# Pooling the first image with half the products, and another order of the work before the main loop

## The chip, the cores and the metric

The program runs on one core of one Trainium2 chip. The metric is the time of one execution on the device in microseconds (us); the median of several runs counts. The profile's names for the engines are PE (TensorE's products), PEld (TensorE's weight loads), DVE (VectorE), ACT (ScalarE), POOL (GpSimd) and SP (SyncE, which issues all transfers here).

## What is computed

Four images of 12,288 queries with 128 channels attend to keys that are pooled from a 384x32 map, and the result goes through a wide layer and back.

```
kv_pool = kv.reshape(B, H // r, r, W // r, r, C).mean(axis=(2, 4))   # r = 4
k = v = kv_pool.reshape(B, -1, C) @ w_sr                             # 768 keys
s = scale * (q @ k.T);  s = s - s.max(-1)
a = exp(s);  a /= a.sum(-1) + 1e-09
x = a @ v                                                            # (49152, 128)
h = x @ w_in                                                         # 2048 wide
out = (0.5 * h * (1 + erf(h / sqrt(2)))) @ w_out                     # 128 wide
```

## The kernel before

**Tiles.** The 49,152 queries are 96 tiles of 512; a tile has four chunks c of 128 queries. The layer's 2048 columns are 16 groups f of 128. All large products are made in float16 with each operand split in a high and a low half, three products for one: `score` (L408, and L439 in halves) for queries by keys, `av_first` (L510) and `av` (L524) for attention by values, `mlp_in` (L543 to L545) and `mlp_out` (L574 to L576) for the layer.

**One tile's path.** `q_max` (L360) and `q_scale` on VectorE find a scale for the queries, `q_split` on GpSimd (L381 to L383) makes the halves, `q_turn` transposes them by a transfer (L389). `score` writes a score chunk, `evac` (L419; `evac_half` L451) takes it out on VectorE with its extreme, `exp` runs on ScalarE (L462), `recips` (L475) makes reciprocals, `attn_hi` and `attn_lo` (L482, L486) make the halves of the attention, `attn_turn` (L495) transposes them by a transfer. `x_out` (L534, L535) makes the layer's input from the product with the values. `gelu` (L557, L559) and `rest` (L563) stand between the layer's two products. `rest(t, p)` serves the groups 2p and 2p + 1.

**Before the first tile.** The first image's map comes in twelve pieces `kv_load(j)` of 512 KB. A piece holds, for each of 128 map rows, two windows w of four pixels e. `kv_pool` (L199) multiplies each pixel's 128x128 float32 block, as the stationary operand, by a 128x32 matrix that averages groups of four rows, and adds four pixels in PSUM. After four pieces ScalarE copies the group out (`kv_copy`, L206), `kv_key` (L212) multiplies by w_sr, and `kv_max` (L218) takes the maximum on VectorE. A short chain on VectorE and TensorE (`kv_bound`, L283 to L297) makes a scale, and `kv_high` and `kv_low` (L303, L308) make the keys' halves.

**The weights.** They arrive as 64-bit numbers in eight chunks, four of w_in (j = 0 to 3) and four of w_out (4 to 7). `w_max` (L632) reads each, `w_scale(i, step)` makes the scale of each matrix, and `w_split(j, step)` makes the two float16 halves in five steps: 0 and 2 on ScalarE (L692, L693, L703), 1 (L695 to L701), 3 (L705, L706) and 4 (L709, L710) on VectorE. Two chunks share one of two staging tiles, so the output weights' transfers wait until the input chunks there have been read.

**What sets the order.** Nothing reorders the work: each engine runs its instructions in the order in which the Python code issues them, and waits only on data and buffers. A list `START` gives that order by hand up to the first layer input of tile 1; behind it a loop over i (tile) and f (group) issues the layer of tile i along with scores and attention of the tiles after it, and `mlp_out` six groups later (`LAG`). In the loop's first turn, i = 1, the dictionary `SECOND` places scores left over from `START`:

```
for name, *a in START:
    by[name](*a)
for i in range(1, NT + 1):
    for f in range(FB if i < NT else LAG):
        if i < NT:
            mlp_in(i, f)
            gelu(i, f)
        if i == 1 and f in SECOND:
            score(*SECOND[f])
            evac(*SECOND[f])
```

## Time and profile before

| | |
|---|---|
| median of 3 runs | 2867.42 us (2867.06 to 2867.5) |
| profiled execution | 2868.9 us, span of the profile 2867.1 us |
| TensorE busy | 2806.6 us (98%) |
| ScalarE busy | 2530.4 us (88%) |
| VectorE busy | 2360.2 us (82%) |
| GpSimd busy | 844.3 us (29%) |

The span runs from the first to the last instruction. Busy shares are averages over the whole of it; the loop over 95 tiles makes up most.

### The profile page before, as it was taken

What the parts mean: (1) busy time and instruction counts of PE and PEld (TensorE: products, weight loads), DVE (VectorE), ACT (ScalarE), POOL (GpSimd) and SP (SyncE); (2) the same over time, 40 slices, a digit from 0 to 9 for tenths busy, and PEclk for the clock granted to TensorE, in tenths of its full rate; (3) what the DMA queues carried; (4) which work ended last, traced back from release to release, by engine and by line L of the source; (5) the groups of instructions that cost most, each with busy time, mean ns of one, the idle gap of its engine ahead of it and who ended that gap; (6) DMA issues with size and microseconds to landing.
All of it is one profiled execution on the core that took longest, in us unless ns stands there. A gap on an engine that the chain in (4) does not pass through costs nothing.

```text
span 2867.1 us, 37928 instructions
## 1 busy us (share of the span) xinstructions
PE 2806.6 (98%) x13570; PEld 1354.0 (47%) x13570; DVE 2360.2 (82%) x3533; ACT 2530.4 (88%) x3416; POOL 844.3 (29%) x801
## 2 busy tenths in 40 slices
PE   7689999999999999999999999999999999999999
PEld 6244444444444444444444444444444444444444
DVE  4778888788878888889788888888878787878785
ACT  2589989898999999999999999999999999999997
POOL 0133433323234334332323344423231323232221
PEclk9899999999999999999999999999999999999999
...
GB/s 176 52 108 117 106 106 112 90 89 101 94 105 109 101 116 116 97 87 103 87 100 98 116 115 109 104 100 85 102 91 100 85 100 85 100 84 101 91 90 48
DMA packets 852990, 284.91 MB, mean 99 GB/s; under 512 B 814656, under 2 KB 817088, under 8 KB 852800
## 3 DMA queue, kind: packets, MB, share of 16 engines
...
q14 instruction: 84, 0.69, 0.1%
...
## 4 chain that ended last, share of the span: by engine, by line
PE 90%; DVE 4%; issue 4%; ACT 1%; DMA 0%; POOL 0%; SPq 0%; POOLq 0%; DVEq 0%; ACTq 0%
PE s L408 12%; PE px L524 12%; PE po L574 11%; PE po L576 11%; PE po L575 11%; PE h L545 11%; PE h L544 11%; PE h L543 11%; DVE gl L563 1%; DVE a L486 1%; DVE a L482 1%; ACT sn L462 1%; DVE sn L419 1%; ACT L462 0%; DMA q<-in_q_dram 0%
## 5 line engine op out<-in xcount | busy, mean ns | idle before, releaser
L557 ACT ACTIVATE g<-h,hs 128x512 f32<-128x512 f32 x1536 | 1006.1, 680 | 235.5 <-PE h L545 214.4
L563 DVE SCALAR_TENSOR_TENSOR gl<-g,gs,gh 128x1024 f16<-128x1024 f32 x768 | 1007.7, 1315 | 39.0 <-ACT gh L559 37.5
L559 ACT ACTIVATE gh<-g,gs 128x1024 f16<-128x1024 f32 x768 | 881.9, 1148 | 25.0
L575 PE MATMUL po<-gl,wo_h 128*128 128x512 f16 x1536 | 582.7, 379 | 4.0 <-DVE gl L563 4.0
L543 PE MATMUL h<-xh,wi_h 128*128 128x512 f16 x1536 | 583.9, 380 | 2.1 <-ACT g L557 1.2
L574 PE MATMUL po<-gh,wo_h 128*128 128x512 f16 x1536 | 582.9, 379 | 2.3 <-ACT oT L581 2.2
L381 POOL TENSOR_TENSOR q<-q,qi 128x512 f32<-128x512 f32 x96 | 100.1, 1043 | 1646.1 <-DVE qi L373 1646.1
L544 PE MATMUL h<-xl,wi_h 128*128 128x512 f16 x1536 | 583.9, 380 | 0.8 <-DVE xl L535 0.8
L545 PE MATMUL h<-xh,wi_l 128*128 128x512 f16 x1536 | 583.9, 380 | 0.0
L576 PE MATMUL po<-gh,wo_l 128*128 128x512 f16 x1536 | 582.6, 379 | 1.1 <-DVE wo_l L710 1.1
L408 PE MATMUL s<-k,q_v 128*128 128x384 f16 x2274 | 434.1, 327 | 25.7 <-DMA q_v<-q_u 12.7
L419 DVE TENSOR_SCALAR_CACHE_REDUCE sn<-s,sg 128x768 f32<-128x768 f32 x379 | 383.7, 1012 | 85.9 <-PE s L408 82.8
L486 DVE SCALAR_TENSOR_TENSOR a<-sn,r,a 128x768 f16<-128x768 f32 x384 | 405.7, 1057 | 13.5
L524 PE MATMUL px<-aT,v 128*128 128x512 f16 x1710 | 416.8, 380 | 0.0
L462 ACT ACTIVATE sn<-sn,nm 128x768 f32<-128x768 f32 x384 | 354.5, 924 | 11.6 <-DVE sn L419 8.9
L408 PEld LDWEIGHTS <-q_v 128*128 128x128 f16 x2274 | 222.5, 98 | 217.1 <-issue 18.2
L524 PEld LDWEIGHTS <-v 128*128 128x128 f16 x1710 | 167.7, 98 | 203.7 <-issue 3.4
L475 DVE TENSOR_SCALAR r<-sum 128x2 f32<-128x2 f32 (+2 forms) x192 | 39.4, 205 | 262.9 <-ACT sn L462 262.9
L482 DVE TENSOR_SCALAR a<-sn,r 128x768 f16<-128x768 f32 x377 | 248.2, 658 | 6.8 <-DVE r L478 0.3
L576 PEld LDWEIGHTS <-wo_l 128*128 128x128 f16 x1536 | 150.4, 98 | 187.7 <-issue 4.4
L545 PEld LDWEIGHTS <-wi_l 128*128 128x128 f16 x1536 | 150.6, 98 | 183.5 <-issue 3.3
L544 PEld LDWEIGHTS <-wi_h 128*128 128x128 f16 x1536 | 150.6, 98 | 179.2 <-issue 4.1
...
## 6 DMA issues: line engine op xcount, KB each, us to landing
...
kv<-in_kv_dram SPq DMA_DIRECT2D x12, 512.0 KB, 9.3
aT<-a SPq DMA_TRANSPOSE x384, 3.2
w<-in_moe_w_in_dram SPq DMA_DIRECT2D x4, 512.0 KB, 5.6
w<-in_moe_w_out_dram SPq DMA_DIRECT2D x4, 512.0 KB, 7.7
q_v<-q_u SPq DMA_TRANSPOSE x96, 2.8
```

Of the source, the lines that this page charges most:

```text
L408: nc.tensor.matmul(ps[:, n, :KH], lhs[:, c], rhs[:, n * KH : (n + 1) * KH], start=rhs is kh and lhs is qh, stop=lhs is ql,)
L486: nc.vector.scalar_tensor_tensor(a[:, 1, :], st.pop(("s", t, c)), st["r", t][:, c : c + 1], a[:, 0, :], op0=ALU.mult, op1=ALU.subtract,)
L524: nc.tensor.matmul(ps, v[:, w, :], aT[:, :, o + k, :], start=k == 0 and i == 0, stop=k == KB - 1 and i == 2,)
L543: nc.tensor.matmul(ps, wi_h[:, fs], xh, start=True, stop=False)
L544: nc.tensor.matmul(ps, wi_h[:, fs], xl, start=False, stop=False)
L545: nc.tensor.matmul(ps, wi_l[:, fs], xh, start=False, stop=True)
L557: nc.scalar.activation(g[:, e, :], ps, AF.Gelu, scale=st["hs", b])
L559: nc.scalar.mul(gh, g, st["gs", b])
L563: nc.vector.scalar_tensor_tensor(gl, st["g", t, p], st["gs", t // TPB], st["gh", t, p], op0=ALU.mult, op1=ALU.subtract)
L574: nc.tensor.matmul(ps, wo_h[:, f, :], gh[:, e, :], start=f == 0, stop=False)
L575: nc.tensor.matmul(ps, wo_h[:, f, :], gl[:, e, :], start=False, stop=False)
L576: nc.tensor.matmul(ps, wo_l[:, f, :], gh[:, e, :], start=False, stop=f == FB - 1)
```

## The change

Four things change, all before or in the loop's first turn.

- A new step `kv_add(j)` adds pixels 2 and 3 of each window to pixels 0 and 1 on VectorE, in place, and `kv_pool` multiplies two blocks a window instead of four.
- The weight steps stand elsewhere: chunks 0 to 2 between the additions, the rest of chunk 2 behind the layer's scale, the rest of chunk 3 among the first tile's layer. The maxima of the output chunks move forward.
- In the first tile, attention chunk 3 is turned and multiplied before chunk 2. The queries of tiles 2 and 3 are scaled earlier, the scores of tile 2 and their exponentials stand in `START`, and so do all products of `mlp_out` of tile 0.
- The loop's first turn starts with the reciprocals of tile 2, and leaves out what `START` now has.

```diff
-    ("w_split", 0, 1), ("w_scale", 0, 2), ("kv_pool", 0), ("w_split", 0, 2), ("w_split", 0, 3),
...
+    ("w_split", 0, 1), ("kv_add", 0), ("kv_pool", 0), ("kv_add", 1), ("kv_pool", 1),
+    ("w_scale", 0, 2), ("w_split", 0, 2), ("kv_add", 2), ("kv_pool", 2), ("w_split", 0, 3),
...
-SECOND = {0: (2, 2), 2: (2, 3), 4: (3, 0), 6: (3, 1), 8: (3, 2), 9: (3, 3)}
+SECOND = {4: (3, 1), 7: (3, 2), 9: (3, 3)}
...
+    def kv_add(j):
+
+        t = st["kv0", j]
+        nc.vector.tensor_tensor(t[:, :, :2], t[:, :, :2], t[:, :, 2:], op=ALU.add)
+
...
-            for e in range(R):
+            for e in range(2):
                 nc.tensor.matmul(
                     st["pp", j // 4][:, o : o + n], t[:, w, e], group,
-                    start=e == 0, stop=e == R - 1,
+                    start=e == 0, stop=e == 1,
                 )
...
-                    if 0 <= k < NT * FB // 2:
+                    if FB // 2 <= k < NT * FB // 2:
                         rest(k // (FB // 2), k % (FB // 2))
-                if i == 1 and f == 3:
-                    exps(2)
+                if i == 1 and f == 0:
                     recips(2)
-                if i == 1 and f in (4, 5, 6, 7):
-                    attn(2, f - 4)
+                    attn(2, 0)
+                    evac(3, 0)
+                if i == 1 and f in (1, 3, 5):
+                    attn(2, (f + 1) // 2)
...
-                    if 0 <= m < NT * FB and (m == n) == (m % FB > 0):
+                    if FB <= m < NT * FB and (m == n) == (m % FB > 0):
                         mlp_out(m // FB, m % FB)
```

The new code stands above most functions, so line numbers rise by 12: L199 becomes L211, L360 becomes L372, L563 becomes L575.

TensorE, the end of the first group's pooling and the first key product, before (`pp` is the pooled group, `kv_j` piece j, `pk` the key product):

```order
L199 MATMUL pp_0_232<-group,kv_2_150 128x32 x8
L199 MATMUL pp_0_232<-group,kv_3_152 128x32 x8
L199 MATMUL pp_1_281<-group,kv_4_154 128x32 x8
L212 MATMUL pk_0_291<-pT_0_276,w_sr_sb 128x256
L199 MATMUL pp_1_281<-group,kv_5_156 128x32 x8
```

The same place in the changed kernel:

```order
L211 MATMUL pp_0_226<-group,kv_2_150 128x32 x4
L211 MATMUL pp_0_226<-group,kv_3_152 128x32 x4
L211 MATMUL pp_1_263<-group,kv_4_154 128x32 x4
L224 MATMUL pk_0_269<-pT_0_256,w_sr_sb 128x256
L211 MATMUL pp_1_263<-group,kv_5_156 128x32 x4
```

The products of a piece are halved, and the order of the pieces and of the key product is the same.

VectorE, from the first weight chunk's selection (`wt`) on, before:

```order
L701 SCALAR_TENSOR_TENSOR wt_193<-wt_193 128x512
L274 TENSOR_REDUCE rho_m<-rho_ps 128x1
L670 TENSOR_SCALAR rmax<-rho_m 128x1
L671 RECIPROCAL xs<-rho_m 128x1
L672 TENSOR_SCALAR xs<-xs,rho 128x1
L705 TENSOR_SCALAR wt_193<-wt_193 128x512
L706 TENSOR_TENSOR wt_193<-wt_193 128x512
L695 TENSOR_SCALAR wt_197<-w_137 128x512
```

and in the changed kernel:

```order
L713 SCALAR_TENSOR_TENSOR wt_193<-wt_193 128x512
L200 TENSOR_TENSOR kv_0_146<-kv_0_146 128x2x256
L200 TENSOR_TENSOR kv_1_148<-kv_1_148 128x2x256
L286 TENSOR_REDUCE rho_m<-rho_ps 128x1
L682 TENSOR_SCALAR rmax<-rho_m 128x1
L683 RECIPROCAL xs<-rho_m 128x1
L684 TENSOR_SCALAR xs<-xs,rho 128x1
L200 TENSOR_TENSOR kv_2_150<-kv_2_150 128x2x256
L717 TENSOR_SCALAR wt_193<-wt_193 128x512
L718 TENSOR_TENSOR wt_193<-wt_193 128x512
L200 TENSOR_TENSOR kv_3_152<-kv_3_152 128x2x256
L707 TENSOR_SCALAR wt_197<-w_137 128x512
```

The additions (L200) stand between the weight steps, and the products of piece j wait for addition j.

VectorE, around the maximum of tile 2's queries (`qm`) in the first tile's layer (`gl` is the result of `rest`, `a` the attention, `sn` scores taken out), before:

```order
L563 SCALAR_TENSOR_TENSOR gl_5_824<-g_10_804,gs_419,gh_10_805 128x1024
L709 SCALAR_TENSOR_TENSOR wt_701<-wt_701,inv_684,wo_h 128x512
L710 SCALAR_TENSOR_TENSOR wo_l<-wt_701,inv_684 128x512
L486 SCALAR_TENSOR_TENSOR a_3_826<-sn_3_638,r_704,a_3_826 128x768
L360 TENSOR_REDUCE qm_842<-q_189 128x4
L369 TENSOR_SCALAR qm_842<-qm_842 128x4
L370 TENSOR_SCALAR qe_844<-qm_842 128x4
L373 TENSOR_SCALAR qi_845<-qe_844 128x4
L397 TENSOR_SCALAR sg_855<-qe_844,ks_401 128x4
L563 SCALAR_TENSOR_TENSOR gl_6_868<-g_12_837,gs_419,gh_12_838 128x1024
L419 TENSOR_SCALAR sn_0_889,nm_887<-s_0_880,sg_855 128x768
```

and in the changed kernel:

```order
L721 SCALAR_TENSOR_TENSOR wt_491<-wt_491,inv_630,wo_h 128x512
L722 SCALAR_TENSOR_TENSOR wo_l<-wt_491,inv_630 128x512
L372 TENSOR_REDUCE qm_662<-q_189 128x4
L381 TENSOR_SCALAR qm_662<-qm_662 128x4
L382 TENSOR_SCALAR qe_664<-qm_662 128x4
L385 TENSOR_SCALAR qi_665<-qe_664 128x4
L575 SCALAR_TENSOR_TENSOR gl_1_680<-g_2_641,gs_379,gh_2_642 128x1024
L498 SCALAR_TENSOR_TENSOR a_0_660<-sn_0_496,r_649,a_0_660 128x768
L409 TENSOR_SCALAR sg_687<-qe_664,ks_360 128x4
L707 TENSOR_SCALAR wt_634<-w_183 128x512
```

The maximum stood behind the sixth `rest` and the last output chunk; it now stands behind the first output chunk and before the second `rest`. The first scores of tile 2 are taken out with 20 rows between, where two rows stood between before.

## Rows read from the trace of the kernel before

**Rows 1.** Busy time in stretches: us, then busy us of PE, PEld, DVE, ACT, POOL (instructions), PEclk.
```profile
12.54:55.26 42.72, 42.72 (x197) 42.22 (x196) 18.66 (x37) 4.16 (x8) 2.80 (x3) 1.00 0.52 179
55.26:81.14 25.88, 17.08 (x124) 10.28 (x125) 18.03 (x60) 13.56 (x25) 0.00 (x0) 1.00 0.47 87
81.14:163.82 82.68, 50.14 (x198) 20.78 (x198) 60.79 (x103) 48.21 (x65) 13.56 (x11) 0.83 0.24 59
...
300.00:1500.00 1200.00, 1198.87 (x5817) 570.57 (x5816) 1020.08 (x1508) 1095.39 (x1477) 382.69 (x357) 1.00 0.44 101
```

**Rows 2.** TensorE in order of time, pooling: start, us, what, [idle before <-releaser].
```profile
12.54 17.11 PE L199 MATMUL pp<-group,kv 128*128 128x32 f32 x80
29.47 1.20 PE L212 MATMUL pk<-pT,w_sr_sb 128*128 128x256 f32 x2
30.46 13.70 PE L199 MATMUL pp<-group,kv 128*128 128x32 f32 x64
...
55.78 1.22 PE L212 MATMUL pk<-pT,w_sr_sb 128*128 128x256 f32 x2 [0.52 <-ACT pT L206]
```

**Rows 3.** VectorE in order of time, same columns: first weight chunk, last key maximum.
```profile
13.02 0.69 DVE L701 SCALAR_TENSOR_TENSOR wt<-wt 128x512 f32<-128x512 f32 x1
...
57.45 0.42 DVE L218 TENSOR_REDUCE mx<-pk 128x1 f32<-128x256 f32 x1 [10.20 <-ACT kT L213]
```

**Rows 4.** VectorE's waits from 81.14 to 163.82: us in total, times, longest us.
```profile
DVE sn L419 <- PE s L408: 7.9, 2, 6.7
DVE r L475 <- ACT sn L462: 6.1, 1, 6.1
DVE xh L534 <- PE px L524: 5.5, 1, 5.5
```

**Rows 5.** TensorE in order of time: scores behind its two longest gaps.
```profile
124.54 2.10 PE L408 MATMUL s<-k,q_v 128*128 128x384 f16 x6 [11.97 <-DMA q_v<-q_u]
...
163.82 1.36 PE L408 MATMUL s<-k,q_v 128*128 128x384 f16 x6 [4.10 <-DVE sn L419]
```

**Rows 6.** GpSimd in order of time: the split of tile 2's queries, and a later one's start.
```profile
117.87 1.04 POOL L381 TENSOR_TENSOR q<-q,qi 128x512 f32<-128x512 f32 x1 [67.60 <-DVE qi L373]
...
120.54 1.15 POOL L383 TENSOR_TENSOR q_u<-q,q_u 128x512 f16<-128x512 f32 x1
...
154.14 1.34 POOL L381 TENSOR_TENSOR q<-q,qi 128x512 f32<-128x512 f32 x1 [13.28 <-DVE qi L373]
```

**Rows 7.** Groups of VectorE's instructions, 81.14 to 163.82: busy us, mean ns | idle before.
```profile
L709 DVE SCALAR_TENSOR_TENSOR wt<-wt,inv,wo_h 128x512 f32<-128x512 f32 x4 | 3.0, 744 | 0.0
...
L706 DVE TENSOR_TENSOR wt<-wt 128x512 f32<-128x512 f32 x4 | 2.8, 692 | 0.2
...
L632 DVE TENSOR_REDUCE wm<-w 128x1 f32<-128x512 f32 x3 | 1.9, 678 | 0.0
...
L705 DVE TENSOR_SCALAR wt<-wt 128x512 int32<-128x512 int32 x4 | 1.7, 420 | 0.0
```

**Rows 8.** VectorE in order of time: `rest` without and beside a split on GpSimd.
```profile
149.92 1.28 DVE L563 SCALAR_TENSOR_TENSOR gl<-g,gs,gh 128x1024 f16<-128x1024 f32 x1
...
157.16 1.92 DVE L563 SCALAR_TENSOR_TENSOR gl<-g,gs,gh 128x1024 f16<-128x1024 f32 x1
```

**Rows 9.** The page's transfers: count, KB each, median us from issue to landing.
```profile
kv<-in_kv_dram SPq DMA_DIRECT2D x12, 512.0 KB, 9.3
aT<-a SPq DMA_TRANSPOSE x384, 3.2
```

**Rows 10.** VectorE in order of time: first score, last weight maximum before x_out(0), x_out(0).
```profile
63.74 1.02 DVE L419 TENSOR_SCALAR_CACHE_REDUCE sn<-s,sg 128x768 f32<-128x768 f32 x1 [0.70 <-PE s L408]
...
78.29 0.68 DVE L632 TENSOR_REDUCE wm<-w 128x1 f32<-128x512 f32 x1
...
81.14 0.75 DVE L534 TENSOR_SCALAR xh<-px,xs 128x512 f16<-128x512 f32 x1 [2.17 <-PE px L510]
```

**Rows 11.** The page's costliest groups: the exponential.
```profile
L462 ACT ACTIVATE sn<-sn,nm 128x768 f32<-128x768 f32 x384 | 354.5, 924 | 11.6 <-DVE sn L419 8.9
```

More of the change, by code (lines that the diff above doesn't have):

```diff
@@ L55 @@
-    ("av_first", 0, 2), ("av_first", 0, 3), ("w_max", 4), ("x_out", 0), ("evac", 1, 3),
-    ("exp", 1, 3), ("mlp_in", 0, 0), ("gelu", 0, 0), ("mlp_in", 0, 1), ("gelu", 0, 1),
-    ("w_max", 5), ("w_max", 6), ("w_max", 7), ("w_scale", 1, 0), ("w_split", 6, 0),
-    ("w_scale", 1, 1), ("w_split", 4, 1), ("mlp_in", 0, 2), ("gelu", 0, 2), ("w_scale", 1, 2),
-    ("out_scale",), ("w_split", 4, 3), ("rest", 0, 0), ("w_split", 4, 2), ("mlp_in", 0, 3),
-    ("gelu", 0, 3), ("w_split", 4, 4), ("w_split", 7, 0), ("recips", 1, 0, 4), ("mlp_in", 0, 4),
@@ L61 @@
-    ("gelu", 0, 4), ("rest", 0, 1), ("w_split", 5, 1), ("mlp_in", 0, 5), ("gelu", 0, 5),
-    ("attn_hi", 1, 0, "act"), ("w_split", 5, 3), ("w_split", 5, 2), ("rest", 0, 2),
-    ("mlp_out", 0, 0), ("mlp_in", 0, 6), ("mlp_out", 0, 1), ("gelu", 0, 6), ("w_split", 5, 4),
-    ("attn_lo", 1, 0), ("attn_turn", 1, 0), ("mlp_out", 0, 2), ("mlp_in", 0, 7), ("gelu", 0, 7),
-    ("w_split", 6, 1), ("rest", 0, 3), ("attn_hi", 1, 1, "act"), ("mlp_out", 0, 3),
-    ("mlp_in", 0, 8), ("w_split", 6, 3), ("w_split", 6, 2), ("gelu", 0, 8), ("attn_lo", 1, 1),
@@ L73 @@
-    ("q_split", 2), ("q_turn", 2), ("q_sigma", 2), ("q_load", 3), ("mlp_out", 0, 8),
-    ("mlp_in", 0, 13), ("gelu", 0, 13), ("rest", 0, 6), ("mlp_out", 0, 9), ("mlp_in", 0, 14),
-    ("gelu", 0, 14), ("score", 2, 0), ("evac", 2, 0), ("mlp_in", 0, 15), ("gelu", 0, 15),
-    ("av", 1, 0), ("av", 1, 1), ("av", 1, 2), ("x_out", 1), ("score", 2, 1), ("evac", 2, 1),
-    ("q_max", 3), ("q_scale", 3), ("q_split", 3), ("q_turn", 3), ("q_sigma", 3),
+    ("evac_half", 1, 2, 0), ("evac_half", 1, 2, 1), ("exp", 1, 2), ("evac", 1, 3),
@@ new lines @@
+    ("exp", 1, 3), ("w_max", 6), ("w_max", 7), ("av_first", 0, 3), ("av_first", 0, 2), ("x_out", 0),
+    ("mlp_in", 0, 0), ("gelu", 0, 0), ("mlp_in", 0, 1), ("gelu", 0, 1),
+    ("w_scale", 1, 0), ("w_scale", 1, 1), ("w_split", 4, 1), ("w_scale", 1, 2), ("out_scale",),
+    ("w_split", 5, 0), ("mlp_in", 0, 2), ("gelu", 0, 2),
+    ("w_split", 4, 3), ("w_split", 4, 2), ("rest", 0, 0), ("recips", 1, 0, 4),
+    ("mlp_in", 0, 3), ("gelu", 0, 3), ("w_split", 4, 4), ("attn_hi", 1, 0, "act"),
+    ("q_max", 2), ("q_scale", 2), ("q_split", 2), ("mlp_in", 0, 4), ("gelu", 0, 4),
@@ new lines @@
+    ("rest", 0, 1), ("attn_lo", 1, 0), ("attn_turn", 1, 0), ("q_turn", 2), ("q_sigma", 2),
+    ("q_load", 3), ("mlp_in", 0, 5), ("gelu", 0, 5), ("w_split", 5, 1),
+    ("mlp_out", 0, 0), ("mlp_in", 0, 6), ("w_split", 5, 2), ("w_split", 5, 3),
+    ("rest", 0, 2), ("w_split", 6, 0),
+    ("mlp_out", 0, 1), ("gelu", 0, 6), ("w_split", 3, 2), ("attn_hi", 1, 1, "act"),
+    ("w_split", 5, 4), ("mlp_out", 0, 2), ("mlp_in", 0, 7), ("gelu", 0, 7), ("w_split", 3, 3),
+    ("w_split", 3, 4), ("rest", 0, 3), ("attn_lo", 1, 1), ("attn_turn", 1, 1),
@@ new lines @@
+    ("score", 2, 0), ("mlp_out", 0, 3), ("mlp_in", 0, 8), ("gelu", 0, 8), ("w_split", 6, 1),
+    ("evac", 2, 0), ("q_max", 3), ("q_scale", 3), ("q_split", 3), ("q_turn", 3), ("q_sigma", 3),
+    ("mlp_out", 0, 4), ("mlp_in", 0, 9), ("gelu", 0, 9), ("attn_hi", 1, 2, "act"),
+    ("w_split", 7, 0), ("rest", 0, 4), ("w_split", 6, 2), ("w_split", 6, 3), ("attn_lo", 1, 2),
+    ("attn_turn", 1, 2), ("mlp_out", 0, 5), ("mlp_in", 0, 10), ("w_split", 6, 4),
+    ("gelu", 0, 10), ("score", 2, 1), ("mlp_out", 0, 6), ("mlp_in", 0, 11), ("gelu", 0, 11),
@@ new lines @@
+    ("attn_hi", 1, 3, "act"), ("rest", 0, 5), ("w_split", 7, 1), ("attn_lo", 1, 3),
+    ("attn_turn", 1, 3), ("evac", 2, 1), ("mlp_out", 0, 7), ("mlp_in", 0, 12), ("gelu", 0, 12),
+    ("w_split", 7, 2), ("w_split", 7, 3), ("w_split", 7, 4), ("mlp_out", 0, 8),
+    ("mlp_in", 0, 13), ("gelu", 0, 13), ("rest", 0, 6), ("mlp_out", 0, 9), ("mlp_in", 0, 14),
+    ("gelu", 0, 14), ("mlp_out", 0, 10), ("mlp_in", 0, 15), ("gelu", 0, 15), ("score", 2, 2),
+    ("evac", 2, 2), ("mlp_out", 0, 11), ("av", 1, 0), ("mlp_out", 0, 12), ("av", 1, 1),
@@ L78 @@
+    ("rest", 0, 7), ("mlp_out", 0, 13), ("av", 1, 2), ("x_out", 1), ("score", 2, 3),
+    ("evac", 2, 3), ("exp", 2, 0), ("exp", 2, 1), ("exp", 2, 2), ("exp", 2, 3),
+    ("mlp_out", 0, 14), ("mlp_out", 0, 15), ("score", 3, 0),
 ]
-SECOND = {0: (2, 2), 2: (2, 3), 4: (3, 0), 6: (3, 1), 8: (3, 2), 9: (3, 3)}
+SECOND = {4: (3, 1), 7: (3, 2), 9: (3, 3)}
 @with_exitstack
```

32 lines of the change are left out of this document (13 added, 19 removed).

## The prediction

> **What bounds the kernel now.** I read the busy time in stretches first, then who waited for whom, then each engine's instructions in order of time for the early part. From 300 to 1500 us it works 1198.87 of 1200 us [rows 1], so one of its instructions ends every 0.206 us (1200 us over 5817) and nothing else can be felt there. That loop is untouched. Time can therefore only be won before TensorE fills up, and a microsecond won there moves everything behind it by one.
>
> Three early stretches have different limits [rows 1]. From 12.54 to 55.26 TensorE is busy all 42.72 us, with pooling products: 192 records of 128x32, 80 of them in 17.11 us [rows 2], so 0.214 us a record and, with two records a product, 0.428 us for each of 96 products. The granted clock is 1.00. VectorE works 18.66 us of that stretch and stands 10.20 us before the last key maximum [rows 3]. From 55.26 to 81.14 a chain runs from the keys to the first tile's input x_out(0). From 81.14 to 163.82 VectorE is busy 60.79 of 82.68 us, TensorE 50.14. Three waits hold 19.5 us of VectorE's idle time: 7.9 on scores, 6.1 on exponentials, 5.5 on the second tile's input [rows 4]; the rest is gaps between instructions and a short wait.
>
> The largest of these starts with the queries of tile 2. Their maximum is taken last on VectorE, so GpSimd begins the split at 117.87, and TensorE stands 11.97 us until the transposed queries land at 124.54 [rows 5, 6]. The second tile's input and exponentials then come late one after the other, until score(3,3) at 163.82, where TensorE stood 4.10 us [rows 5]. From that instruction on both kernels have the same TensorE order, so the change is worth what it moves score(3,3).
>
> **A. Pooling.** 48 products of 96 go, 48 x 0.428 = 20.5 us of TensorE. Twelve additions of 128x512 in float32 come to VectorE; the nearest row is the addition's sibling L706 (float32, two tensors in SBUF, the same size), 0.69 us [rows 7], started every 0.62. The first addition stands behind the selection that starts at 13.02 and holds the queue 0.6 us [rows 3], so TensorE starts at about 14.3 instead of 12.54. From there 20.5 us of products and two key products at 0.99 us (29.47 to 30.46) give 36.8. VectorE's list between these points is 7.4 us of additions, 0.7 for the scale, 9.9 of weight splitting (its steps at 0.42 to 0.74 [rows 7]), 0.7 for two maxima, and about 2 us of waiting for the keys of groups 0 and 1: the last addition is done near 34.4, and the last products need it near 35.5. So it hardly waits; I allow 0.5 us and the copy's 0.52. The third key product starts at 37.8, not 55.78 [rows 2]: **-18.0 us**. Bounds: with additions that cost nothing -18.5; with additions as long as the next larger VectorE operation, 1.28 us for 128x1024 [rows 8], the list grows by 7.9, of which 1.1 is slack, so -11. I take 0.62 since size, type and memory are those of L706. The inputs take 9.3 us to land [rows 9] from issues at 4 to 16 us, ahead of the additions. The weight pieces that are now split later are covered by the wait before the last maximum, except two. The first is the second product of chunk 2, put before the first score evacuation: two instructions, L709 at 0.74 [rows 7] and its like, beside an idle time of 0.70 there, before 63.74 [rows 10]. The second is the remainder of chunk 3, moved into the third stretch: counted in C. The maxima of output chunks 0 and 1 go into waits of VectorE in the bound's chain. The third and fourth output weights now load only after chunk 3 has left its staging tile, near 37.5 instead of 26; SyncE's queue holds one query load and the value transpose (due at 44.5) behind them, and they are read near 60: nothing.
>
> **B. Keys to x_out(0).** The second product adds 0 to 0.75 us, and I take 0.4, since a later wait absorbs the rest. Turning chunk 3 before chunk 2 lets its transpose (3.2 us to landing [rows 9]) start about 1 us earlier, so the last one lands about 1 us sooner after the same attention work. But the evacuation of (1,3) and two weight maxima now stand before x_out(0): from 78.29, 0.95 + 2 x 0.62, later by 0.4, gives 80.9 against 81.14 [rows 10]. **-0.2 us**, bounds -1.4 (the transpose alone decides) and +1.5 (all shifts add).
>
> **C. x_out(0) to score(3,3).** VectorE's work there changes by three maxima (1.9 [rows 7]) and one evacuation (0.95) out, and the rest of chunk 3 (0.42 + 0.69 + twice 0.74, 2.5 by starts) in: -0.3. Now the waits. The queries of tile 2 are scaled behind the first output chunk instead of behind the last. Their split on GpSimd (3.8 us, 117.87 to 121.7 [rows 6]) and transpose (2.8 us more, to 124.54) then run beside some 14 us of other VectorE work that stands ahead of evac(2,0): the longest wait, 6.7 us, goes. The scores of tile 2 are spread among the products of tile 0, and the other score wait goes as well. Two remain. Before x_out(1): behind the last attn_lo(1,3) a transpose must land (3.2) and 24 matmuls run (24 x 0.206 = 5.0); VectorE has 6.9 us of work in that time (two evacuations at 0.95, two of rest at 1.2, one pair of each later split step), so it waits 1.5. The granted clock was 0.83 over this stretch [rows 1], and six score products took 2.10 us after the 11.97 us gap against 1.36 after the 4.10 us gap [rows 5]; I add 0.8 for matmuls at the lower of the clock's two levels (1.2 and 2.4 GHz), 2.3 together. Before the reciprocals of tile 2: one exponential (0.92 [rows 11], and its read-out), 1.2. So 3.5 us for 19.5.
>
> Against this, the splits of tiles 2 and 3 on GpSimd now lie beside a full VectorE queue. Beside the split from 154.14 [rows 6], one VectorE operation took 1.92 against 1.28 us [rows 8]; with two operations hit per split, 1.3 each, half of it inside the wait before x_out(1): +1.3. Sum: -19.5 + 3.5 - 0.3 + 1.3 = **-15.0 us**; bounds -18.5 (no wait remains) and -7 (8 us more of waits).
>
> On the same row the Trainium skill has a rule, SBUF — State Buffer, section "SBUF: two separate sides": a VectorE operation with two SBUF inputs and a GpSimd operation that reads SBUF exclude each other, and the later one blocks for the whole instruction. This speaks against the change. By it each of the two splits could hold VectorE for its full 3.7 us; the sum would be about 5 us worse than with the row's 0.64 per operation.
>
> **Sum.** -18.0 - 0.2 - 15.0 = -33.2. The profiled execution took 2868.9 us around a span of 2867.1; it lies 1.5 above the median 2867.42. The sum gives 2835.7 from the one and 2834.2 from the other: **2835**.
>
> **The rivals.**
> - *Additions late* (0.08). VectorE's queue, not TensorE, paces the pooling. For it: only 1.1 us of slack by the list. Against: the row of the same size and type is 0.69 us, not 1.28. With 1.28 us an addition, 2842.
> - *The waits only move* (0.15). TensorE, ScalarE and VectorE now wait on each other in short turns in tile 0: ScalarE has the high half of chunk 5 in its queue before GELU 6, and must wait for VectorE's selection there; x_out(1) stands behind transposes and slow matmuls. With 8 us more of waits, 2843.
> - *The port* (0.05). GpSimd's splits block VectorE for 3.7 us each instead of stretching single operations, 2 x 3.7 for 2 x 1.3: 2840.
> - *Only the pooling pays* (0.06). Term C comes to nothing: 2868.9 - 18.2 = 2851, or 2849 against the median.
> - *Slower* (0.04). The loop does not fill up again: with one aT buffer and one score buffer, a wait that the new start sets up recurs in each of some 93 tiles. It decides from 0.43 us a tile ((33.2 + 5.7) / 93); at 0.6 us the time is 2890. Against: TensorE idles 1.1 us in 1200 [rows 1] and VectorE is busy 1020, ScalarE 1095 of those, so both can catch up some 2.5 us a tile.
> - *Nothing changes* (0.02). The products wait for additions so long that pooling ends where it did, and the queries' wait stays: 2867.
>
> **How the numbers follow.** The forecast as worked out, within 2827 to 2841, has 0.60. With the late additions, moved waits and the port, 0.88 lies within 2826 to 2847, which is the range: its lower end takes nearly all the best bounds of the terms (some 5 us), its upper the moved waits and one late term. Faster by over 0.2% (5.7 us, about what can be told from no change) holds in all cases but the last two: 0.94; same 0.02; slower 0.04.
>
> **What would show it.** Pooling: 96 records still 0.214 us apart, the third key product near 38, additions near 0.69 us. B: x_out(0) near 63. C: no wait above 3 us on VectorE between x_out(0) and score(3,3), which starts near 131; named waits of VectorE of 3 to 4 us in all. GpSimd: its splits of tiles 2 and 3 before 100. Loop: TensorE full as before from about 135 on. Wrong would make it: products further apart than 0.214 us, a gap of TensorE above 5 us behind the tile-2 scores or before x_out(1), or idle TensorE in later tiles.

## The result

The changed kernel takes 2834.96 us (median of 3 runs, 2834.48 to 2835.08) against 2867.42 before: a ratio of 0.9887, with a 95% interval of 0.9864 to 0.9909. 2835 was predicted. The profiled execution took 2835.08 us around a span of 2833.3, so the span fell by 33.8 us from 2867.1.

The same three stretches in the changed kernel, and the same piece of the loop, cut at the same instructions as in [rows 1]: the first pooling product, the third key product (in [rows 1] the cut is 0.52 us ahead of it), x_out(0) and score(3,3). Columns are as there.

```profile
14.59:38.32 23.73, 22.96 (x101) 22.12 (x101) 20.83 (x40) 3.31 (x8) 2.17 (x3) 1.00 0.67 233
38.32:63.17 24.85, 17.75 (x124) 10.60 (x125) 22.34 (x68) 13.11 (x24) 1.41 (x1) 1.00 0.58 143
63.17:130.59 67.42, 45.66 (x197) 19.70 (x197) 62.67 (x103) 48.90 (x67) 13.35 (x10) 0.95 0.34 77
300.00:1500.00 1200.00, 1198.79 (x5817) 570.62 (x5815) 1020.70 (x1503) 1096.08 (x1477) 384.29 (x357) 1.00 0.44 101
```

The reader sees first that the loop is as full as it was. Then that VectorE (the third busy figure) now works 20.83 of 23.73, 22.34 of 24.85 and 62.67 of 67.42 us: it was the busiest engine of the second and third stretches before as well (70% and 74% of them, [rows 1]) and now fills 90% and 93% of them, and in the first it comes close to TensorE.

| | before | after | difference | predicted |
|---|---|---|---|---|
| third key product starts | 55.78 | 38.32 | -17.46 | -18.0 (A) |
| from there to x_out(0) | 25.36 | 24.85 | -0.51 | -0.2 (B) |
| x_out(0) to score(3,3) | 82.68 | 67.42 | -15.26 | -15.0 (C) |
| behind score(3,3), to the span's end | 2703.28 | 2702.71 | -0.57 | 0 |
| span | 2867.1 | 2833.3 | -33.8 | -33.2 |

TensorE in order of time, the pooling that answers to [rows 2] and the scores that answer to [rows 5]:

```profile
14.59 8.74 PE L211 MATMUL pp<-group,kv 128*128 128x32 f32 x40 [1.61 <-DVE kv L200]
23.15 1.20 PE L224 MATMUL pk<-pT,w_sr_sb 128*128 128x256 f32 x2
24.14 5.43 PE L211 MATMUL pp<-group,kv 128*128 128x32 f32 x24
...
32.45 5.35 PE L211 MATMUL pp<-group,kv 128*128 128x32 f32 x24
...
38.32 1.22 PE L224 MATMUL pk<-pT,w_sr_sb 128*128 128x256 f32 x2 [0.52 <-ACT pT L218]
...
81.15 2.10 PE L420 MATMUL s<-k,q_v 128*128 128x384 f16 x6 [5.07 <-DMA q_v<-q_u]
...
130.59 1.14 PE L420 MATMUL s<-k,q_v 128*128 128x384 f16 x6 [2.82 <-DVE sn L431]
```

96 records remain (40, 24, 8 and 24; the row of 8 starts at 29.75 and isn't shown), still 0.214 us apart ((23.15 - 14.59) / 40), and after the first one no wait for an addition (`kv`, L200) stands there. The 11.97 us in front of tile 2's scores have become 5.07.

VectorE's waits from 63.17 to 130.59, which answer to [rows 4]: 3.0 us for 19.5.

```profile
DVE xh L546 <- PE px L536: 1.9, 1, 1.9
DVE r L487 <- ACT sn L474: 1.1, 1, 1.1
```

GpSimd in order of time, the splits of the queries of tiles 2 and 3, which answer to [rows 6]. Both lie before 100; the split of tile 2 starts at 73.68 for 117.87.

```profile
73.68 2.00 POOL L393 TENSOR_TENSOR q<-q,qi 128x512 f32<-128x512 f32 x1 [33.95 <-DVE qi L385]
75.75 1.22 POOL L394 CAST q_u<-q 128x512 f16<-128x512 f32 x1
77.05 1.28 POOL L395 TENSOR_TENSOR q_u<-q,q_u 128x512 f16<-128x512 f32 x1
...
92.16 2.14 POOL L393 TENSOR_TENSOR q<-q,qi 128x512 f32<-128x512 f32 x1 [13.83 <-DVE qi L385]
```

VectorE in order of time: two additions, the last key maximum (10.20 us of waiting before it in [rows 3], 1.26 now), x_out(0) without a wait, and operations beside the two splits, which answer to [rows 8].

```profile
33.44 1.28 DVE L200 TENSOR_TENSOR kv<-kv 128x512 f32<-128x512 f32 x2
...
39.98 0.42 DVE L230 TENSOR_REDUCE mx<-pk 128x1 f32<-128x256 f32 x1 [1.26 <-ACT kT L225]
...
63.17 0.74 DVE L546 TENSOR_SCALAR xh<-px,xs 128x512 f16<-128x512 f32 x1
...
74.70 1.80 DVE L498 SCALAR_TENSOR_TENSOR a<-sn,r,a 128x768 f16<-128x768 f32 x1
76.42 0.57 DVE L409 TENSOR_SCALAR sg<-qe,ks 128x4 f32<-128x4 f32 x1
76.91 0.41 DVE L707 TENSOR_SCALAR wt<-w 128x512 int32<-128x512 int32 x1
77.36 1.52 DVE L710 SCALAR_TENSOR_TENSOR wt<-w,wt 128x512 int32<-128x512 int32 x1
...
93.32 1.26 DVE L717 TENSOR_SCALAR wt<-wt 128x512 int32<-128x512 int32 x1
94.61 0.98 DVE L718 TENSOR_TENSOR wt<-wt 128x512 f32<-128x512 f32 x1
95.52 1.91 DVE L498 SCALAR_TENSOR_TENSOR a<-sn,r,a 128x768 f16<-128x768 f32 x1
```

The same operations take 1.01 (L498), 0.22 (L409), 0.69 (L710), 0.42 (L717) and 0.69 (L718) where GpSimd stands still, so the first split costs VectorE 0.79 + 0.35 + 0.83 = 2.0 us and the second 0.84 + 0.29 + 0.90 = 2.0.

### The profile page after: what moved, and what is told of

Its sections match the earlier page's. It is cut to its first block, busy times and chain, and to the rows that moved or that the text cites. A ratio compares the mean times of both kernels' runs of the same rounds, so it can differ in the third digit from the quotient of the medians.

```text
span 2833.3 us, 37750 instructions
## 1 busy us (share of the span) xinstructions
PE 2782.8 (98%) x13474; PEld 1333.2 (47%) x13474; DVE 2373.6 (84%) x3545; ACT 2530.6 (89%) x3416; POOL 844.4 (30%) x801
## 4 chain that ended last, share of the span: by engine, by line
PE 92%; DVE 6%; ACT 1%; issue 1%; DMA 0%; SPq 0%; DVEq 0%; ACTq 0%
PE s L420 12%; PE px L536 12%; PE po L586 11%; PE po L588 11%; PE po L587 11%; PE h L557 11%; PE h L555 11%; PE h L556 11%; DVE gl L575 1%; DVE a L498 1%; DVE sn L431 1%; PE pp L211 1%; DVE a L494 1%; ACT sn L474 0%; DMA w<-in_moe_w_in_dram 0%
## 5 line engine op out<-in xcount | busy, mean ns | idle before, releaser
L575 DVE SCALAR_TENSOR_TENSOR gl<-g,gs,gh 128x1024 f16<-128x1024 f32 x768 | 1010.1, 1318 | 37.5 <-ACT gh L571 36.1
L431 DVE TENSOR_SCALAR_CACHE_REDUCE sn<-s,sg 128x768 f32<-128x768 f32 x379 | 383.9, 1013 | 74.5 <-PE s L420 70.4
L498 DVE SCALAR_TENSOR_TENSOR a<-sn,r,a 128x768 f16<-128x768 f32 x384 | 407.7, 1062 | 13.4
```

Source lines behind the costliest of these rows:

```text
L498: nc.vector.scalar_tensor_tensor(a[:, 1, :], st.pop(("s", t, c)), st["r", t][:, c : c + 1], a[:, 0, :], op0=ALU.mult, op1=ALU.subtract,)
L575: nc.vector.scalar_tensor_tensor(gl, st["g", t, p], st["gs", t // TPB], st["gh", t, p], op0=ALU.mult, op1=ALU.subtract)
```

## The experiments

Eleven kernels ran, in three groups, each with runs of the kernel before beside it on the same chip (medians 2868.24, 2868.32 and 2867.96). The changed kernel's ratio makes 2835.8 and 2835.9 of the first two; in the third it ran itself. The first pooling product starts between 14.1 and 15.2 us in these profiles, whatever was edited behind it (16.31 in the first experiment, and 12.69 in the second, which has no additions); for effects of 3 us and less I therefore count from that product. From there the changed kernel reaches the third key product after 23.73, x_out(0) after 48.58 and score(3,3) after 116.00 us.

**1. The sums alone.** The kernel before, with each addition put right ahead of its piece's products and every other step where it was.

```diff
-    ("w_split", 0, 1), ("w_scale", 0, 2), ("kv_pool", 0), ("w_split", 0, 2), ("w_split", 0, 3),
+    ("w_split", 0, 1), ("w_scale", 0, 2), ("kv_add", 0), ("kv_pool", 0), ("w_split", 0, 2), ("w_split", 0, 3),
...
-            for e in range(R):
+            for e in range(2):
```

> The kernel before with the twelve additions and half the products, each addition right before its products, and everything else in the old order. My theory: TensorE needs 20.5 us less for pooling, but in the old order the additions stand behind whole weight steps, so VectorE's queue paces the later pieces; by the durations of the changed kernel's rows the third key product starts near 44.4 instead of 55.8, and everything behind it moves by that: 2856 us (2853 to 2860). Rival, the pooling's gain is TensorE's alone, whatever the order: third key product near 38, 2850. Rival, the gain comes from the other order and the sums give nothing: within 5 us of 2867.

Measured: 2856.82 us, ratio 0.9962 [0.9947, 0.9976]. TensorE in order of time:

```profile
19.91 1.91 PE L204 MATMUL pp<-group,kv 128*128 128x32 f32 x8 [1.68 <-DVE kv L193]
23.02 5.33 PE L204 MATMUL pp<-group,kv 128*128 128x32 f32 x24 [1.20 <-DVE kv L193]
...
33.90 3.62 PE L204 MATMUL pp<-group,kv 128*128 128x32 f32 x16 [1.15 <-DVE kv L193]
...
45.40 1.22 PE L217 MATMUL pk<-pT,w_sr_sb 128*128 128x256 f32 x2 [0.52 <-ACT pT L211]
```

The products wait for additions four times (1.68, 1.20, 1.15 and 1.17, the last at 41.26), 5.2 us in all, and the first product starts at 16.31 for 14.59, since the weight scale's last step now stands ahead of the addition. 5.2 and 1.7 make 6.9 of the 7.1 us by which the key product comes later than in the changed kernel. The rival of the late additions is a real mechanism then: with weight steps in the old places it takes 7 of the 17.5 us. The steps between the additions are a part of term A, not decoration.

**2. The order alone.** The changed kernel without the additions, with four products a window.

```diff
-    ("w_split", 0, 1), ("kv_add", 0), ("kv_pool", 0), ("kv_add", 1), ("kv_pool", 1),
+    ("w_split", 0, 1), ("kv_pool", 0), ("kv_pool", 1),
...
-            for e in range(2):
+            for e in range(R):
```

> The changed kernel without the additions, with all 96 pooling products, and all of the new order. My theory: pooling ends as before (third key product near 55.8), and only the two later terms remain, 0.5 and 15.3 us: 2851 us (2849 to 2854), with x_out(0) to score(3,3) near 67.4 us. Rival, the new order pays only because pooling left VectorE free earlier: 2860 or more. Rival, the queries' and scores' order is worth all of the gain and the sums little: below 2843.

Measured: 2852.51 us, ratio 0.9949 [0.9933, 0.9966]; third key product at 55.93, x_out(0) 24.85 us behind it, score(3,3) 67.44 us behind that. Terms B and C stand to 0.02 us (24.85 and 67.42 in the changed kernel) with term A gone, so they don't hang on it. The two parts alone give -11.4 and -15.7; together -27.1 of some -32.4. The other 5.3 us need both at once. What they are, the first experiment's rows show: its key product comes 7.1 us later than the changed kernel's, 5.2 of that in waits for additions. The medians are not sharp enough to tell 5.3 from 7.1, since the runs of each of these two kernels spread over 2.2 and 4.6 us.

**3. The queries late.** The changed kernel with the maximum, scale and split of tile 2's queries where the splits of output chunk 1 are over, ahead of the first scores of tile 2.

```diff
-    ("q_max", 2), ("q_scale", 2), ("q_split", 2), ("mlp_in", 0, 4), ("gelu", 0, 4),
-    ("rest", 0, 1), ("attn_lo", 1, 0), ("attn_turn", 1, 0), ("q_turn", 2), ("q_sigma", 2),
-    ("q_load", 3), ("mlp_in", 0, 5), ("gelu", 0, 5), ("w_split", 5, 1),
+    ("mlp_in", 0, 4), ("gelu", 0, 4),
+    ("rest", 0, 1), ("attn_lo", 1, 0), ("attn_turn", 1, 0),
+    ("mlp_in", 0, 5), ("gelu", 0, 5), ("w_split", 5, 1),
...
+    ("q_max", 2), ("q_scale", 2), ("q_split", 2), ("q_turn", 2), ("q_sigma", 2), ("q_load", 3),
     ("score", 2, 0), ("mlp_out", 0, 3), ("mlp_in", 0, 8), ("gelu", 0, 8), ("w_split", 6, 1),
```

> The changed kernel with the scaling, split and transpose of tile 2's queries (and the load of tile 3's) moved back to right before the first scores of tile 2. My theory: the chain from their maximum over GpSimd (some 4 us) and the transpose (2.8) stands open again, and VectorE has only one weight step (1.8 us) to put beside it: a wait of about 6.5 us before evac(2,0) and one or two more behind it, 2843 us (2841 to 2846). Rival, the lead of the queries is not what closed the gap, since VectorE's queue is full anyway: 2835 to 2837.

Measured: 2841.87 us, ratio 0.9908 [0.9893, 0.9922], 6.1 above the changed kernel. TensorE's first scores of tile 2, and VectorE's waits from x_out(0) to score(3,3):

```profile
93.38 2.10 PE L421 MATMUL s<-k,q_v 128*128 128x384 f16 x6 [17.29 <-DMA q_v<-q_u]
```

```profile
DVE sn L432 <- PE s L421: 5.9, 1, 5.9
DVE gl L576 <- ACT gh L572: 4.1, 2, 3.9
DVE xh L547 <- PE px L537: 1.9, 1, 1.9
DVE r L488 <- ACT sn L475: 1.1, 1, 1.1
```

The old wait on the scores is back (5.9 us, 6.7 in [rows 4]), with its cause beside it: TensorE stands 17.29 us on the transposed queries. VectorE waits 13.0 us for 3.0, and the stretch takes 74.77 us (63.83 to 138.60) for 67.42. Of the 10 us more of waits 7.35 show, since the splits cost VectorE less: tile 3's now lies inside the wait of 3.9 us and stretches nothing, and tile 2's hits two operations for 1.0 us.

**4. More work on GpSimd.** The changed kernel with eight float32 multiplications of 128x512, on a tile of their own, behind the split of tile 3.

```diff
-    ("attn_turn", 1, 2), ("mlp_out", 0, 5), ("mlp_in", 0, 10), ("w_split", 6, 4),
+    ("attn_turn", 1, 2), ("idle_work", 8), ("mlp_out", 0, 5), ("mlp_in", 0, 10), ("w_split", 6, 4),
...
+            nc.gpsimd.tensor_tensor(spare, spare, spare, op=ALU.mult)
```

> The changed kernel with eight extra float32 multiplications of 128x512 on GpSimd, on a tile of their own that nothing waits for, behind the split of tile 3's queries in the first tile's layer. My theory: GpSimd's work stretches VectorE's operations with two inputs in SBUF; in the changed kernel two splits of 2.8 us alone cost VectorE some 4.0 us, 0.71 per us, so 8.3 us alone cost 5.9, of which 1.9 fall into the wait before x_out(1): 2839 us (2837 to 2841). Rival, each GpSimd instruction blocks VectorE for its whole length: 2841.4 or more. Rival, no contention: 2835.

Measured: 2842.29 us, ratio 0.9912 [0.9897, 0.9927], 6.5 above the changed kernel. That is outside the 2837 to 2841 that I expected, and inside what the rival expected (2841.4 or more). The stretch takes 73.74 us for 67.42. GpSimd, and VectorE beside it, in order of time:

```profile
97.40 12.40 POOL L730 TENSOR_TENSOR spare<-spare 128x512 f32<-128x512 f32 x8
```

```profile
101.06 2.06 DVE L575 SCALAR_TENSOR_TENSOR gl<-g,gs,gh 128x1024 f16<-128x1024 f32 x1
103.04 1.26 DVE L707 TENSOR_SCALAR wt<-w 128x512 int32<-128x512 int32 x1
104.33 1.41 DVE L710 SCALAR_TENSOR_TENSOR wt<-w,wt 128x512 int32<-128x512 int32 x1
...
108.83 1.00 DVE L431 TENSOR_SCALAR_CACHE_REDUCE sn<-s,sg 128x768 f32<-128x768 f32 x1
```

Seven of VectorE's operations (98.17 to 107.11) take 0.66 to 0.84 us longer, whether they take 0.42 us alone (L707) or 1.28 (L575), 5.3 us together. L431, whose scores come from PSUM, is not hit. The eight multiplications take 12.4 us, 1.55 each, where GpSimd's float32 operation of that size takes 1.04 alone [rows 6]. So in this stream the price goes by the operation, about 0.75 us for each that meets a GpSimd operation, and my price by the microsecond was too low. The other 1.0 us is the wait before x_out(1), 2.9 for 1.9. It need not be GpSimd's: the six score products ahead of it, at 109.89, took 2.06 us for 1.14, at a granted clock of 0.64 from 100 to 112. By its time the rival did better than my theory, though 1.3 us of this profile lie ahead of the added work (x_out(0) 49.84 us behind the first product for 48.58; see experiment 6). By its rows VectorE was not held for the full length of the GpSimd work, since it lost 5.3 us beside 12.4. I read them as two engines that take turns, one operation each; no run tests that by itself.

**5. The two attention chunks.** The changed kernel with chunk 2 turned and multiplied before chunk 3, as before.

```diff
-    ("attn_turn", 0, 3), ("attn_turn", 0, 2), ("score_half", 1, 2, 0), ("score_half", 1, 2, 1),
+    ("attn_turn", 0, 2), ("attn_turn", 0, 3), ("score_half", 1, 2, 0), ("score_half", 1, 2, 1),
...
-    ("exp", 1, 3), ("w_max", 6), ("w_max", 7), ("av_first", 0, 3), ("av_first", 0, 2), ("x_out", 0),
+    ("exp", 1, 3), ("w_max", 6), ("w_max", 7), ("av_first", 0, 2), ("av_first", 0, 3), ("x_out", 0),
```

> The changed kernel, with the first tile's attention chunk 2 turned and multiplied before chunk 3 again, as before. My theory (term B: turning chunk 3 first lets the last transpose land about 1 us earlier, while later evacuations and maxima take part of that back): x_out(0) 0.5 to 1.1 us later, so behind the third key product 25.4 to 26.0 us for 24.85, and the time up by as much, below what a time can tell. Rival (the order of the two chunks hides behind VectorE's other work): 24.7 to 25.0.

Measured, in one run: 2835.79 us, and x_out(0) 25.47 us behind the third key product (37.92 to 63.39), 0.62 more than in the changed kernel, both at a granted clock of 1.00. It waits 0.55 us on the last product there, where the changed kernel has none:

```profile
63.39 0.75 DVE L546 TENSOR_SCALAR xh<-px,xs 128x512 f16<-128x512 f32 x1 [0.55 <-PE px L522]
```

By these two profiles the order of the chunks is worth 0.6 us, a little more than all of term B (0.51).

**6. One product a window in the last group.** The changed kernel with a second addition (pixel 1 onto pixel 0) for pieces 8 to 11.

```diff
+        if j >= 8:
+            nc.vector.tensor_tensor(t[:, :, :1], t[:, :, :1], t[:, :, 1:2], op=ALU.add)
...
-            for e in range(2):
+            for e in range(1 if j >= 8 else 2):
```

> The changed kernel, with a second addition (pixel 1 onto pixel 0) in the pieces 8 to 11 of the first image, so that these take one product a window instead of two. 8 products of 0.428 us go, 3.4 us of TensorE; 4 additions of 0.42 us or less come, before the last products need them. My theory (TensorE's products bound the pooling; the additions keep up): the third key product at 35.4 to 36.4 for 38.32, and all behind it earlier by 1.9 to 2.9, the time lower by 1.9 to 2.9. Rival (VectorE's queue is already the pace in the last group, so the products wait for the second additions): third key product at 37.5 or later, gain below 0.8.

Measured: 2835.24 us, ratio 0.9884 [0.9870, 0.9899], no gain that can be told. The third key product is at 36.49, but from the first product that is 22.30 for 23.73, 1.4 us where 1.9 to 2.9 was expected: the last products wait 0.89 us for a second addition. And x_out(0) comes 49.25 us behind the first product, 0.7 *later* than in the changed kernel. TensorE in order of time, and two stretches ahead of x_out(0) (columns as in [rows 1]):

```profile
33.84 2.13 PE L213 MATMUL pp<-group,kv 128*128 128x32 f32 x8 [0.89 <-DVE kv L202]
...
58.89 2.12 PE L422 MATMUL s<-k,q_v 128*128 128x384 f16 x6
```

```profile
52.00:58.00 6.00, 3.73 (x34) 3.02 (x33) 5.83 (x15) 3.35 (x6) 0.00 (x0) 0.74 0.79 180
58.00:63.50 5.50, 5.40 (x53) 4.24 (x51) 4.35 (x15) 4.02 (x9) 0.00 (x0) 0.67 0.43 93
```

The granted clock (the figure behind the five engines) is 0.74 and 0.67 there, means with a part of the time at the lower of its two levels (1.2 and 2.4 GHz), where the changed kernel's first profile had 1.00 in both; six score products take 2.12 us for 1.14, and VectorE waits 0.9 us on them. TensorE had been idle for longer just before: 2.28 us ahead of the product of the key bound (39.99), for 1.43. Whether that is why the clock fell, the ninth experiment asks.

Three other profiles bear on it. Up to x_out(0) the code of experiments 3, 4 and 7 is the changed kernel's, without a second addition, and TensorE's idle time ahead of the key bound is the changed kernel's too (1.43, 1.44 and 1.43 us). Their clock fell all the same, in the fourth experiment by as much:

```profile
52.00:58.00 6.00, 3.48 (x30) 2.63 (x29) 5.83 (x15) 3.40 (x6) 0.00 (x0) 0.78 0.67 153
58.00:63.50 5.50, 5.50 (x53) 4.46 (x52) 4.46 (x16) 3.81 (x7) 0.00 (x0) 0.62 0.56 122
```

It was 1.00 and 0.69 in the third and 0.99 and 0.70 in the seventh. The six score products took 2.13, 2.12 and 1.68 us, VectorE waited 0.7, 1.0 and 0.5 us on them, and x_out(0) came 49.37, 49.84 and 49.12 us behind the first product. So neither the fall of the clock nor the late x_out(0) needs the second addition, and the 0.7 us are no measure of it.

**7. The queries of tile 4 earlier.** The changed kernel with tile 4's queries loaded in the start and scaled and split in VectorE's wait before x_out(1), instead of in the loop's first turn, and score(2,3) with its evacuation ahead of that product's last chunk.

```diff
+    ("q_load", 4),
...
-    ("rest", 0, 7), ("mlp_out", 0, 13), ("av", 1, 2), ("x_out", 1), ("score", 2, 3),
-    ("evac", 2, 3), ("exp", 2, 0), ("exp", 2, 1), ("exp", 2, 2), ("exp", 2, 3),
+    ("rest", 0, 7), ("mlp_out", 0, 13), ("q_max", 4), ("q_scale", 4), ("q_split", 4),
+    ("score", 2, 3), ("evac", 2, 3), ("av", 1, 2), ("x_out", 1), ("exp", 2, 0), ("exp", 2, 1), ("exp", 2, 2), ("exp", 2, 3),
```

> The changed kernel, with the queries of tile 4 loaded in the start and scaled and split in VectorE's wait before x_out(1), and score(2,3) and its evacuation ahead of the last product for x_out(1). My theory (in the third stretch VectorE's busy time sets the end, and its two named waits, 3.0 us, can be filled): from x_out(0) to score(3,3) 63.5 to 65 us for 67.42, time lower by 2.4 to 3.9. Rival (GpSimd's split of tile 4, now beside VectorE's full queue, stretches two or three operations by 0.7 us each and the wait moves elsewhere): 66.4 us or more, gain of 1 us or less.

Measured: 2831.15 us (2830.20 to 2833.84), ratio 0.9872 [0.9858, 0.9887]. From x_out(0) to score(3,3) it is 64.26 us (64.06 to 128.32) for 67.42. VectorE's waits between:

```profile
DVE sn L432 <- PE s L421: 0.3, 1, 0.3
DVE xh L547 <- PE px L537: 0.3, 1, 0.3
```

0.6 us for 3.0. Of the 3.2 us, 2.4 are idle time that was filled, and 0.8 are contention: in the changed kernel this split stands at 125.91, still ahead of score(3,3), and stretches two operations there by 1.0 us (see C below), while at its new place (111.81 to 114.77) it stretches none. The stretch came out as expected (63.5 to 65). The time fell by some 4.8 us, more than the 2.4 to 3.9 expected.

**8. Both of these.** The second addition and the early queries of tile 4.

```diff
+        if j >= 8:
+            nc.vector.tensor_tensor(t[:, :, :1], t[:, :, :1], t[:, :, 1:2], op=ALU.add)
...
+    ("q_load", 4),
...
+    ("rest", 0, 7), ("mlp_out", 0, 13), ("q_max", 4), ("q_scale", 4), ("q_split", 4),
```

> The second addition for pieces 8 to 11 and the earlier queries of tile 4 together. My theory: the two stretches follow each other, so the gains add: score(3,3) at 124 to 127 for 130.59, 4.3 to 6.8 us lower than the changed kernel, ratio to the kernel before 0.9863 to 0.9872. Rival (either one only moves a wait): 1 to 3 us lower, ratio 0.9877 to 0.9884.

Measured: 2832.23 us (2829.92 to 2833.34), ratio 0.9873 [0.9856, 0.9889]: 3.7 below the changed kernel, between the rival's 1 to 3 and my 4.3 to 6.8. My sum missed. x_out(0) is 49.25 us behind the first product, as in the sixth, at a clock of 0.75 and 0.66; score(3,3) follows 64.61 us later, as in the seventh. The second addition adds nothing that the time shows.

**9. TensorE kept busy.** The sixth kernel with eight products whose results nobody reads, in TensorE's idle time around the key bound.

```diff
-    ("kv_add", 11), ("kv_pool", 11), ("kv_copy", 2), ("kv_key", 2), ("q_max", 1),
+    ("kv_add", 11), ("kv_pool", 11), ("kv_copy", 2), ("kv_key", 2), ("spare", 5), ("q_max", 1),
...
-    ("kv_max", 2), ("kv_bound", 0), ("kv_bound", 1), ("w_max", 4), ("kv_bound", 2),
+    ("kv_max", 2), ("kv_bound", 0), ("kv_bound", 1), ("spare", 3), ("w_max", 4), ("kv_bound", 2),
...
+            nc.tensor.matmul(ps[:, :32], w_sr_sb, group, start=True, stop=True)
```

> The kernel with the second addition for pieces 8 to 11, and with eight products of a 128x128 float32 block by 32 columns, whose results nobody reads, put into TensorE's idle time there: five behind the third key product (it stood 2.28 us) and three behind the product of the key bound (1.85 us). My theory (the second addition's gain was lost since TensorE, idle for longer, ran the scores of (1,3) and the last attention products at a granted clock of 0.74 and 0.67 from 52 to 63.5 us, where the changed kernel had 1.00): with the idle time filled the clock stays near 1.00 there, the six score products (1,3) take 1.14 us for 2.12, VectorE's wait of 0.91 us on them goes, and x_out(0) starts 0.8 to 1.2 us earlier against the first pooling product (48.0 to 48.5 us behind it, for 49.25). Rival (VectorE's own queue and the transposes set x_out(0), the clock does not): 49.0 us or more, whatever the clock.

Measured: 2835.83 us, ratio 0.9887 [0.9872, 0.9902], with a first product at 15.21. The same two stretches:

```profile
52.00:58.00 6.00, 3.01 (x29) 1.91 (x27) 5.83 (x16) 3.94 (x8) 0.00 (x0) 1.00 0.58 131
58.00:63.50 5.50, 4.47 (x60) 3.67 (x60) 5.43 (x17) 4.24 (x9) 0.00 (x0) 1.00 0.65 146
```

The clock is back at 1.00, the six scores take 1.14 us, VectorE's wait on them is gone, and x_out(0) comes 48.05 us behind the first product: 1.2 before the sixth kernel and 0.5 before the changed one, as expected. The late start and the half microsecond's size hide this in the time. But the clock was 1.00 in the changed kernel's first profile as well, without these products, so this profile doesn't show that they kept it there. What it shows is the second addition at a clock of 1.00 on both sides: 48.05 for 48.58, a gain of 0.5 us.

**10. All of it.** The eighth kernel with the ninth's eight products.

```diff
+    ("spare", 5),
...
+    ("spare", 3),
...
+    ("q_max", 4), ("q_scale", 4), ("q_split", 4),
```

> The second addition, the same eight products in TensorE's idle time, and the earlier queries of tile 4. My theory: the gains of the first stretch (0.8 to 1.2 us) and of the third (3.2 us) add: from the first pooling product to score(3,3) 112.2 to 112.9 us, for 116.0 in the changed kernel and 113.9 with the second addition and the queries alone. Rival (the first stretch's gain is lost again before score(3,3)): 113.5 or more.

Measured: 2831.54 us (2831.24 to 2831.87), ratio 0.9872 [0.9856, 0.9889]. score(3,3) comes 113.33 us behind the first product, outside what I expected (112.2 to 112.9) and short of the rival's 113.5. In this profile the clock was 0.93 and 0.77 in the two stretches, though the program up to there is the ninth's; x_out(0) came after 48.73. So the idle time alone doesn't settle the clock. What holds in all four profiles with the second addition is that x_out(0) follows it: 49.25 at 0.74 and 0.67, 49.25 at 0.75 and 0.66, 48.73 at 0.93 and 0.77, 48.05 at 1.00 and 1.00.

**11. The changed kernel again**, beside the ninth and tenth, without any edit.

> The changed kernel itself, once more, on the chip on which the others of this call run. By its first runs 0.9887 of the kernel before: 2835 to 2837 here; it says what 3 to 4 us between the variants are worth. A second time below 2833 would say that the variants' gains are within what two chips differ by.

Measured: 2835.50 us (2835.35 to 2835.82), ratio 0.9886 [0.9871, 0.9901]; third key product, x_out(0) and score(3,3) 23.73, 48.58 and 116.02 us behind the first product, as in its first profile. The seventh and tenth kernels, at 2831.15 and 2831.54, are thus some 4 us better than the changed kernel: no run of theirs comes within 1.5 us of its runs here, though the intervals of the ratios overlap, and the seventh ran on another chip, on which the kernel before took 0.4 us more.

## Why the prediction was right, by its own steps

**What bounds.** That time could only be won before TensorE fills up held: of the 33.8 us by which the span fell, 33.2 lie before score(3,3), and 0.6 behind it. The runs show that this last part is scatter: from score(3,3) to the end it is 2700.5, 2703.7 and 2702.8 us in the profiles of experiments 6, 9 and 11, whose code is the same from there on.

**A, pooling** (-17.46 for -18.0). The half of the products went at the price per record that was read, and the additions at 0.62 us by starts (33.44 to 34.64 for two). Of the 0.5 us missing, 0.3 stand ahead of the first product (14.59 for 14.3). That the additions "hardly wait" was right for this order and only for it: the first experiment shows 5.2 us of such waits with the weight steps in the old places, and the sixth shows 0.89 us as soon as VectorE gets four short additions more. The 1.1 us of slack was a fair reading of a queue that was nearly full: VectorE works 20.83 of the 23.73 us.

**B, keys to x_out(0)** (-0.51 for -0.2). Right between profiles at the same clock: 1.00 before, in the changed kernel, and in the fifth experiment, which gives 0.6 us to the order of the chunks. But in experiments 3, 4 and 7, whose code is the same up to there, this stretch took 25.65, 26.11 and 25.40 us, at mean clocks of 0.93, 0.87 and 0.93 and with VectorE waiting 0.5 to 1.0 us on the scores of (1,3). So from profile to profile it moves by more than term B gives (the changed kernel's second profile, at 0.93, lost nothing: 24.85). No term of the prediction had that; its upper bound of +1.5 covers it.

**C, x_out(0) to score(3,3)** (-15.26 for -15.0). The split of tile 2 early enough is what pays, shown by taking it back alone: the third experiment loses 7.35 of the 15.26 us in this stretch, with the old wait back in its place. Which of the moved scores and exponentials gave the other 7.9 us no experiment takes apart; the second shows that they belong to the order and not to the additions. The two waits that were forecast to remain are the two that remain, 1.9 us for 2.3 before x_out(1) and 1.1 for 1.2 before the reciprocals. The first of them is near by luck: the scores there ran at the upper clock level (1.14 us for six products at 103.77 and 111.25), so the 0.8 us for a low clock was not paid, and the rest of the wait was 1.9 for 1.5 (by its own figures 8.2 less 6.9, which is 1.3). VectorE's idle time fell by 17.14 us (21.89 to 4.75), of which the named waits make 16.5, and its busy time grew by 1.88.

The one term that was mis-sized is the contention with GpSimd, where I had "two operations hit per split, 1.3 each, half of it inside the wait": +1.3. It measured three operations and 2.0 us for each of the two splits, and nothing of it lay inside a wait. A third split, that of tile 4, lies in this stretch in both kernels. In the changed one it stretched two operations:

```profile
126.38 1.68 DVE L498 SCALAR_TENSOR_TENSOR a<-sn,r,a 128x768 f16<-128x768 f32 x1
127.98 1.62 DVE L575 SCALAR_TENSOR_TENSOR gl<-g,gs,gh 128x1024 f16<-128x1024 f32 x1
```

They take 1.02 and 1.28 alone, 1.0 us less, so the stretch holds 5.0 us of contention in all. But I had counted the kernel before as free of it, which it wasn't. Groups of VectorE's instructions there, 81.14 to 163.82 (columns as in [rows 7]):

```profile
L563 DVE SCALAR_TENSOR_TENSOR gl<-g,gs,gh 128x1024 f16<-128x1024 f32 x12 | 16.6, 1384 | 0.7 <-ACT gh L559 0.6 <-issue 0.2
L486 DVE SCALAR_TENSOR_TENSOR a<-sn,r,a 128x768 f16<-128x768 f32 x8 | 9.0, 1124 | 0.1
```

Against 1.28 and 1.01 alone that is 1.2 us for `rest` and 0.9 for `attn_lo`; one `attn_hi` (0.96 for 0.61) makes it 2.5. So the net is 2.5 us, for 1.3 forecast, and the rest of VectorE's work shrank by 0.6, for 0.3. In all, busy time came out 0.9 worse than forecast (+1.88 for -0.3 and +1.3) and idle time 1.1 better (0.5 in the named waits, 0.6 in the gaps between instructions, which I had left alone): the two misses cancelled, and C came out closer than its working deserved.

**Small slips of the working.** (33.2 + 5.7) / 93 is 0.42 us a tile, not 0.43. The range's lower end, 2826, lies 9 us below the forecast, while the best bounds of the terms make 5.2. Neither moved the forecast.

**The rivals.** *Additions late* did not happen here and does happen with another order (experiment 1). *The waits only move*: the place that I named was right, since ScalarE's high halves wait 8.2 us on VectorE's selections, 4.5 of them in front of one in chunk 5; but VectorE had other work there, and lost nothing. The gap of 5.07 us before tile 2's first scores just passes the 5 us that I had named as a sign against me, and cost nothing either: these scores are done at 83.3, and VectorE comes to take them out at 89.78. *The port*: GpSimd's splits cost 2 x 2.0 us, between my 2 x 1.3 and the rival's 2 x 3.7. The Trainium skill ("SBUF — State Buffer", section "SBUF: two separate sides") says that the engine which starts first keeps the shared port for the whole instruction. The rows agree with this by the instruction, not by the split: both sides get longer, VectorE's operations by 0.66 to 0.84 us, which is less than one GpSimd operation alone (1.04), and GpSimd's from 1.04 to 1.55 (experiment 4). *Only the pooling pays*, *slower* and *nothing changes* are excluded by -15.3 in C, by a loop as full as before, and by a third key product 17.5 us earlier.
